# Attention and soft mixture of experts on one core: every place in the written order drawn anew, and the dummy products ahead of the weights' product

## The chip, the core and the metric

The kernel runs on one core of a Trainium2 chip. The core has five engines with a queue each: PE (matrix products), DVE and POOL (vector work), ACT (scalar functions, here exponentials and copies with a cast) and SP, which here only starts transfers. The metric is the device time of one execution in microseconds (us), as the median of several runs. Every time below is of the kernel before.

## The reference, cut to what matters

For each of 4 batches there are 12,288 queries of 128 channels. The keys and values are the same 768 vectors: 12,288 inputs averaged in blocks of 4 x 4 and multiplied by a 128 x 128 matrix.

```python
kv_pool = kv.reshape(B, H // r, r, W // r, r, C).mean(axis=(2, 4))
k = v = kv_pool.reshape(B, -1, C) @ w_sr
s = scale * (q @ k.transpose(0, 2, 1))
a = np.exp(s - s.max(-1, keepdims=True)); a /= a.sum(-1, keepdims=True) + 1e-09
x = (a @ v).reshape(B * S, C)
logits = x @ phi                                  # 32 slots
d = np.exp(logits - logits.max(0)); d /= d.sum(0) + 1e-09
slot_in = d.T @ x                                 # over all 49,152 rows
slot_out = (per expert: relu(slot_in @ w1) @ w2)  # 8 experts of 4 slots
c = np.exp(logits - logits.max(1, keepdims=True)); c /= c.sum(1, keepdims=True) + 1e-09
out = c @ slot_out
```

The second softmax goes over all rows of all batches, so the result can only be written once every query has been seen. The kernel needs the attention output x only through its logits and through slot_in, and never forms it: it works from the probabilities.

## The kernel before, in words

The 49,152 queries are 384 tiles of 128, and 12 tiles make a group: 32 groups, g0 to g31, 8 to a batch. Of tile number i in a group (0 to 11) these steps are made:

- **s** (L499 to L501, PE): six products of 128 x 384, the scores of 128 queries against 768 keys, in three passes (high and low parts of both sides).
- **m** (L505, L506, DVE): the row maximum of the scores. **e** (L514, ACT): the exponential with its row sums.
- Half of each tile's probabilities is turned for the next product by DVE (**tr**, L538), the other half is cut into a high half-precision part on ACT for two tiles at once (**hi**, L521), a low part on POOL (**lo**, L525) and turned by a transposing transfer from SP (**pd**, L534, into the tile pb). hi5 serves the tiles 10 and 11, and lo10, lo11, pd10 and pd11 follow it.

Of a group:

- **LA** and **LB** (L575, L587, PE): the logits from the two halves. LB reads pb, so it needs the group's last transposing transfer to have landed.
- **lev** (L596, L598): copies of the sums out of the accumulator; **lsel** (L604, PE) puts them together; **ltr** (L613, DVE) turns them; **ln** (L632, POOL) divides by the row sums.
- **mcol** (L638, DVE) and **mmm** (L644, PE): the column maximum over the group; **mred** (L649, L659, DVE): the running maximum. **dsub** (L665, POOL), **dexp** (L702, ACT), **dmul** (L710, POOL): the weights of the second softmax.
- **T0** to **T5** (L725, PE): these weights times the probabilities, two tiles in each piece, accumulated by **tacc** (L736, DVE).
- **cmax**, **csub**, **cexp** (L741, L744, L747): the numerators of the third softmax, kept or spilled.

The steps of a group are spread over the two groups that follow: while PE does the scores of group g it does LA, LB and lsel of g-1 and the T pieces of g-1 and g-2. During a batch the keys of the next one are made: loads (L352), adds on POOL and DVE (L356), products and their evictions (**kmm** L364, **khi** L367, **klo** L371, **umm** L379, **vmm** L424). After the last group come the experts and the output.

The head, before the first tile, loads the first batch's inputs in two halves, pools them on POOL and DVE (L296, L300), and makes the keys: **hkmm0** and **hkmm1** (L364) for the two halves, **hkx** (L467) for two pieces that skip the pooling adds, **hklo0** and **hklo1** (L371) on DVE. **hfla** is 50 products of the identity with itself into a bank that nobody reads (L265). **hw** is one product of the layer's matrix with phi (L276), and **hwo** its eviction on ACT.

The order on PE, DVE, ACT and POOL is written out by hand: each step is recorded with a time `at` (the tile that it belongs to) and a kind, and the table TAU holds a number for each kind. The steps are issued in the order of the sum; a step never comes ahead of one that it needs:

```python
key = at + TAU.get(kind, 0.0)
for d in deps:
    key = max(key, self.ops[d][2] + 1e-4)
...
for n in sorted(range(len(self.ops)), key=lambda n: (self.ops[n][2], n)):
    self.ops[n][4]()
```

Kinds with an `a` ahead stand for the first group of the program, with `y` and `z` for the last two, where they differ. SP is not under this order: the framework places its transfers. A step that waits holds back everything behind it on its engine.

Of the kernel before, what the change touches and what calls it, by code (L numbers as in the profile page):

```python
# [31 lines left out]
    "ka9": -265.483, "am2": -228.979, "ka26": -228.315, "ka27": -216.005, "hkx1": -210.101, "wl6": -205.889,  # L32
    "aT5": -200.576, "aql2": -199.988, "cmul3": -193.632, "kv1": -192.138, "hkhi0": -189.577, "alo5": -188.166,
    "klo1": -184.904, "am4": -184.036, "am11": -176.431, "am6": -174.783, "cmul7": -173.78, "cmul13": -166.529,
    "crec24": -162.887, "alev0": -161.94, "humm1": -160.171, "ka28": -158.796, "hlad": -153.938, "atr2": -149.703,
    "apd9": -145.014, "hlat1": -141.493, "cmul9": -140.13, "csum13": -136.466, "hklo0": -129.179, "ka4": -128.974,
    "as8": -128.908, "aLB2": -126.414, "hqh": -126.33, "humax": -125.006, "as11": -122.356, "ahi1": -121.758,
    "humm0": -121.346, "hkx2": -121.032, "ka21": -120.235, "umm1": -119.793, "atr1": -116.116, "alo1": -114.554,
    "crec9": -113.922, "ceps12": -113.76, "am7": -113.033, "crec21": -112.6, "csum28": -111.014, "ceps30": -108.21,
    "cmul11": -106.687, "ka8": -104.178, "apd1": -102.343, "xho12": -102.266, "wl4": -102.002, "xht14": -99.953,  # L40
    "apd4": -99.229, "csum12": -97.996, "as1": -96.721, "hkmm0": -95.947, "wl3": -95.195, "aql1": -94.09,
    "ka20": -92.708, "admul": -92.617, "alo4": -91.302, "ae3": -91.262, "ahi4": -90.444, "s7": -89.221,
    "ys7": -89.221, "apd5": -88.975, "kd3": -88.752, "zs7": -88.656, "amcol": -87.304, "aqd1": -87.275, "m2": -86.508,
    "zm2": -86.508, "ym2": -86.384, "alo3": -83.039, "ae8": -82.636, "e7": -82.523, "ye7": -82.523, "ze7": -82.367,
    "ka10": -81.698, "huout": -81.585, "aLB0": -80.918, "ae10": -80.428, "cmul17": -80.252, "ahi3": -79.401,
    "xso22": -78.357, "alo11": -77.577, "ahi5": -77.082, "s1": -76.481, "zs1": -76.481, "pd2": -76.281,
    "ypd2": -76.281, "zpd2": -76.281, "ka5": -76.232, "cmul2": -76.128, "m6": -75.891, "ym6": -75.891, "ys1": -75.891,
    "husc": -74.638, "zm6": -74.521, "alo7": -73.738, "csum1": -73.624, "ceps13": -73.102, "hfla": -70.294,
    "ae5": -69.588, "ka13": -67.698, "csum22": -67.308, "csum0": -65.39, "am1": -65.188, "as3": -64.589,
    "amred": -63.833, "lev1": -63.476, "ylev1": -63.476, "zlev1": -63.476, "cb1": -62.918, "csum27": -62.889,  # L50
    "cmul15": -62.49, "hvout0": -61.708, "as5": -59.277, "ceps25": -59.027, "hkmm1": -57.375, "wl5": -54.296,
    "zs0": -54.296, "s0": -54.234, "ys0": -54.044, "as0": -53.451, "adexp": -53.316, "cmul16": -53.122,
    "am10": -52.657, "ceps9": -52.634, "ceps1": -52.622, "ae6": -51.993, "wl0": -51.933, "ceps31": -51.12,
# [114 lines left out]
def attention_then_soft_moe(ctx: ExitStack, tc: tile.TileContext, E, qT, kv0, kvT, w_sr, w_srT, phi, w1, w2, outT, spill):  # L168
# [78 lines left out]
    op = plan.op  # L247
# [5 lines left out]
    pT = pm.tile([P, 512], F32, tag="pT", name="pT")  # L253
# [24 lines left out]
    def w_out():  # L278
        nc.scalar.activation(
            wp4, D.pop("pw")[:, :NS].unsqueeze(1).broadcast_to([P, NQD, NS]), AF.Copy, scale=1.0 / R2  # L280
        )

    a = op("PE", "hw", -90, [], w_mm, acq=[("x", "pw")])
    ops_w = op("ACT", "hwo", -90, [a], w_out, use=[("x", "pw")])

    raw = {}
# [817 lines left out]
    a = None  # L1104
# [119 lines left out]
```

## Time and profile before

| what | value |
| --- | --- |
| time, median of 3 runs | 949.61 us (948.67 to 954.53) |
| the profiled execution | 953.79 us, of which the trace spans 952.0 us |
| PE busy | 860.9 us (90% of the span) |
| DVE, POOL, ACT busy | 792.9, 697.4, 667.0 us (83%, 73%, 70%) |
| mean granted clock of PE | 0.98 of 2.4 GHz |
| transposing transfers | 384, median 3.2 us from issue to landing |

Busy time is an average over stages. The head takes about the first 48 us, the main loop with its 31 groups runs to about 840 us, the last group's end, the experts and the output follow. In a row of waits the engine and line that waited stand first, and behind the arrow what ended last before it could go on; "issue" there means that the profile names nothing. A transfer's duration on SP is only the time that its issue takes; when its data has landed is told apart.

### The profile page before, as it was taken

How to read it: one execution, taken by the hardware profiler on the slowest of the kernel's cores; microseconds unless marked ns; L12 is line 12 of the kernel's file. 1: busy time of each engine (PE TensorE's matmuls, PEld its weight loads, DVE VectorE, ACT ScalarE, POOL GpSimd, SP SyncE). 2: the span in 40 equal slices, each digit the busy share in tenths (PEclk: the TensorE clock that was granted, in tenths of full speed). 3: DMA queues.
4: the chain of work that ended last, by engine and by line, in shares of the span. 5: the costliest groups of instructions: out<-in, count | busy, mean ns of one | idle time of the engine just before them, and what ended most of it. 6: DMA issues, size and time to landing. Idle time of an engine off the chain costs nothing. (4 is left out here: it accounts for less than half of the span.)

```text
span 952.0 us, 27485 instructions
## 1 busy us (share of the span) xinstructions
PE 860.9 (90%) x10616; PEld 634.1 (67%) x10616; DVE 792.9 (83%) x1497; ACT 667.0 (70%) x1253; POOL 697.4 (73%) x822
## 2 busy tenths in 40 slices
PE   6798999989999999989999999899999999967882
PEld 6666776766777776657777777667777777744341
DVE  3887898988998988889999989888989798945891
ACT  1586787867887777767888778767878787831562
POOL 4377799886788888876787989957877677746530
PEclk9999999999999999999999999999999999989985
DMA  8377798997888899866888889867867767697699
GB/s 322 98 129 140 134 183 194 179 170 143 148 160 169 174 169 201 168 135 131 154 162 154 165 180 173 157 108 135 131 133 135 122 127 139 114 257 291 275 412 374
DMA packets 338867, 167.64 MB, mean 176 GB/s; under 512 B 310832, under 2 KB 313648, under 8 KB 338608
## 3 DMA queue, kind: packets, MB, share of 16 engines
q1 hardware_dynamic: 337728, 162.59, 79.2%
q10 hardware_dynamic: 1008, 3.29, 0.9%
q8 instruction: 83, 1.36, 0.6%
q14 instruction: 48, 0.39, 0.1%
HBM read 62.01 MB, written 28.31 MB: 95 GB/s over the span
## 5 line engine op out<-in xcount | busy, mean ns | idle before, releaser
L514 ACT ACTIVATE p<-s,nm 128x768 f32<-128x768 f32 x384 | 344.1, 897 | 124.6 <-DVE nm L506 113.6
L525 POOL TENSOR_TENSOR hl<-p,hl 128x384 f16<-128x384 f32 x384 | 347.6, 926 | 75.9 <-ACT hl L521 75.7
L505 DVE TENSOR_REDUCE nm<-s 128x1 f32<-128x768 f32 x384 | 363.6, 947 | 30.3 <-PE s L501 29.5
L499 PE MATMUL s<-khi,qhi 128*128 128x384 f32 x768 | 280.2, 365 | 8.1 <-ACT p L514 5.7
L501 PE MATMUL s<-khi,qlo 128*128 128x384 f32 x768 | 258.7, 337 | 0.2 <-POOL qlo L483 0.2
L500 PE MATMUL s<-klo,qhi 128*128 128x384 f32 x768 | 258.0, 336 | 0.2 <-DVE klo L371 0.2
L499 PEld LDWEIGHTS s<-khi,qhi 128*128 128x128 f32 x768 | 143.9, 187 | 75.0 <-issue 42.3
L538 DVE STREAM_TRANSPOSE pa<-p 128x768 f32<-128x768 f32 x192 | 176.7, 945 | 0.5 <-ACT p L514 0.2
L521 ACT ACTIVATE hl<-p 128x768 f16<-128x768 f32 x192 | 157.5, 836 | 17.0 <-DMA pb<-hl 13.8
L725 PE MATMUL pT<-p,D 128*32 128x192 f32 x3072 | 146.0, 332 | 2.8 <-POOL D L710 2.5
L500 PEld LDWEIGHTS s<-klo,qhi 128*128 128x128 f32 x768 | 144.5, 188 | 1.1 <-DVE klo L371 0.4
L501 PEld LDWEIGHTS s<-khi,qlo 128*128 128x128 f32 x768 | 144.1, 188 | 0.6 <-POOL qlo L483 0.5
L483 POOL TENSOR_TENSOR qlo<-q,qhi 128x512 fp32r<-128x512 f32 x96 | 124.7, 1299 | 5.8 <-ACT qhi L479 5.8
L725 PEld LDWEIGHTS pT<-p,D 128*32 128x32 f32 x3072 | 91.1, 110 | 44.4 <-POOL D L710 11.0
L575 PE MATMUL lq<-pa,vu 32*32 32x384 f32 x3072 | 88.4, 491 | 2.7 <-ACT hl L521 2.4
L587 PE MATMUL lq<-pb,vb 128*32 128x384 f16 x1152 | 56.1, 339 | 22.3 <-DMA pb<-hl 14.7
L514 ACT ACTIVATION_READ_ACCUMULATOR p<-s,nm 128x1 f32 x384 | 74.1, 193 | 0.0
L506 DVE TENSOR_SCALAR nm<-nm 128x1 f32<-128x1 f32 x384 | 59.0, 154 | 13.2
L598 DVE COPY lps<-lq 128x768 f32<-128x768 f32 x32 | 30.7, 958 | 47.0 <-PE lq L587 47.0
L356 POOL TENSOR_TENSOR LL<-LL 128x384 f32<-128x384 f32 x66 | 65.1, 1010 | 5.1 <-DVE LL L356 5.1
L632 POOL TENSOR_TENSOR LL<-LL,ri 128x384 f32<-128x384 f32 x32 | 26.6, 833 | 56.5 <-DVE LL L613 37.5
L587 PEld LDWEIGHTS <-vb 128*32 128x32 f16 x1152 | 30.3, 99 | 56.3 <-issue 36.6
(131 smaller groups left out, 822.4 us busy)
## 6 DMA issues: line engine op xcount, KB each, us to landing
q<-qT SPq DMA_DIRECT2D x96, 256.0 KB, 3.1
outT<-o SPq DMA_DIRECT2D x32, 768.0 KB, 11.1
LL<-kvT SPq DMA_DIRECT2D x48, 384.0 KB, 3.8
pb<-hl SPq DMA_TRANSPOSE x384, 3.2
raw<-kv SPq DMA_DIRECT2D x6, 768.0 KB, 7.9
w_p<-w SPq DMA_DIRECT2D x6, 768.0 KB, 7.4
pa<-w SPq DMA_DIRECT2D x1, 3328.0 KB, 16.7
spill<-LL SPq DMA_DIRECT2D x16, 192.0 KB, 3.5
```

Of the source, the lines that this page charges most:

```text
L483: nc.gpsimd.tensor_tensor(out=lo, in0=src, in1=hi.bitcast(F32), op=ALU.subtract)
L499: nc.tensor.matmul(s, hi[:, qc], khi[:, k], start=True, stop=False)
L500: nc.tensor.matmul(s, hi[:, qc], klo[:, k], start=False, stop=False)
L501: nc.tensor.matmul(s, lo[:, qc], khi[:, k], start=False, stop=True)
L505: nc.vector.tensor_reduce(out=NM[t], in_=S[t][:, :, :HK], axis=XY, op=ALU.max, negate=True)
L514: nc.scalar.activation(PP[t // 2][:, t % 2, :].rearrange("p (h n) -> p h n", h=2), S.pop(t)[:, :, :HK], AF.Exp, bias=NM.pop(t), scale=1.0, ...
L521: nc.scalar.activation(HL[k][:, :, 0, :], PP[k][:, :, KA:], AF.Copy)
L525: nc.gpsimd.tensor_tensor(out=hl[:, 1, :], in0=PP[t // 2][:, t % 2, KA:], in1=hl[:, 0, :], op=ALU.subtract)
L538: nc.vector.transpose(out=PA[:, n, :, o : o + 2, :].rearrange("p n a i -> p a n i"), in_=PP[k][:, :, :KA].rearrange("p a (n j) -> p a n j" ...
L575: nc.tensor.matmul(lp(g, c, r), VU[b][rows, kb, :], PA[rows, halves(g), kb, :, :], start=(k == 0), stop=False, skip_group_check=True)
L587: nc.tensor.matmul(lp(g, c, r), VB[b][:, w, kb, :], PB[:, halves(g), p * NBB + kb, :, r * Q32 : (r + 1) * Q32], start=False, stop=(n + NQD ...
L725: nc.tensor.matmul(d["pst"][c * Q32 : (c + 1) * Q32, :KW], d["D"][:, t, :], pp[:, u, c * KW : (c + 1) * KW], start=(t == 0), stop=(t == G ...
```

## The change

It does two things. All numbers of TAU are replaced, so most steps stand in another place; the numbers were found by a search that reckons with a longer landing of the transposing transfers. And in the head the 50 dummy products are issued first on PE, with the weights' product hw behind them (it now depends on them), where hw was first before. No step is added or taken away, and no step's shape changes. In the changed kernel line numbers are 19 higher from the table's end to the new lines, and 20 higher behind them.

```diff
 TAU = {
-    "ka9": -265.483, "am2": -228.979, "ka26": -228.315, "ka27": -216.005, "hkx1": -210.101, "wl6": -205.889,
...
+    "crec24": -162.887, "crec21": -112.6, "csum28": -111.014, "ceps30": -108.21, "ae3": -85.272053, "cmul17": -80.252,
...
-    a = op("PE", "hw", -90, [], w_mm, acq=[("x", "pw")])
+    a = op("PE", "hfla", 0, [], lambda: fill(pT, 50), acq=[("T", "f0")])
+    a = op("PE", "hw", -90, [a], w_mm, acq=[("x", "pw")])
     ops_w = op("ACT", "hwo", -90, [a], w_out, use=[("x", "pw")])
...
-    op("PE", "hfla", 0, [], lambda: fill(pT, 50), acq=[("T", "f0")])
+
     kv_ops(0, 0, [[pool0[0]], [pool0[1]]], [("p", "po0")], "h")
```

Three places matter for what follows.

First, DVE in a group in the middle of the loop, from the maxima that follow LB to mred. L505 and L506 are one tile's maximum (s is its scores), L613 ltr, L638 and L639 mcol, L649 and L659 mred. Before:

```order
699 L505 TENSOR_REDUCE nm_6308<-s_6299 128x1
700 L506 TENSOR_SCALAR nm_6308<-nm_6308 128x1
701 L613 STREAM_TRANSPOSE LL<-px 128x384
702 L505 TENSOR_REDUCE nm_6331<-s_6324 128x1
703 L506 TENSOR_SCALAR nm_6331<-nm_6331 128x1
704 L638 TENSOR_REDUCE cq_6348<-LL 128x12
705 L639 TENSOR_REDUCE cm_6349<-cq_6348 128x1
706 L505 TENSOR_REDUCE nm_6370<-s_6334 128x1
707 L506 TENSOR_SCALAR nm_6370<-nm_6370 128x1
708 L649 TENSOR_REDUCE gm_6380<-px 128x32
709 L659 TENSOR_TENSOR gm_6380<-gm_6380,gm_6011 128x32
```

Now (L525 and L526 the maximum, L633 ltr, L658 and L659 mcol, L669 and L679 mred, L643 the reciprocals that ln needs):

```order
701 L525 TENSOR_REDUCE nm_6312<-s_6305 128x1
702 L526 TENSOR_SCALAR nm_6312<-nm_6312 128x1
703 L643 RECIPROCAL ri_6315<-r_5681 128x12
704 L633 STREAM_TRANSPOSE LL<-px 128x384
705 L525 TENSOR_REDUCE nm_6341<-s_6334 128x1
706 L526 TENSOR_SCALAR nm_6341<-nm_6341 128x1
707 L658 TENSOR_REDUCE cq_6348<-LL 128x12
708 L659 TENSOR_REDUCE cm_6349<-cq_6348 128x1
709 L525 TENSOR_REDUCE nm_6365<-s_6358 128x1
710 L526 TENSOR_SCALAR nm_6365<-nm_6365 128x1
711 L669 TENSOR_REDUCE gm_6376<-px 128x32
712 L679 TENSOR_TENSOR gm_6376<-gm_6376,gm_6009 128x32
```

The pattern is the same, but each of ltr, mcol and mred now stands behind the maximum of a tile one later: 8, 9 and 10 where it was 7, 8 and 9. On PE the same shift shows as LB, s6, s7, s8, lsel, s9, s10, s11, mmm, T4, T5, s0, s1, T0, where it was LB, s6, s7, lsel, s8, s9, s10, mmm, T4, T5, s11, s0, s1, T0 (T4 and T5 of the group before, s0 and s1 of the group after). So T0 stands two tiles behind mmm and no longer three.

Second, POOL in the same group, from dsub to the lows of the last tiles. L525 is a low part (x2: two tiles), L665 dsub, L710 dmul, L483 a query's low part, L744 csub, L619 a step of the row sums. Before:

```order
311 L665 TENSOR_TENSOR D_6383<-LL,gm_6380 128x384
312 L525 TENSOR_TENSOR hl_6373<-p_6306,hl_6373 128x384
313 L710 TENSOR_TENSOR D_6383<-D_6383,ri_6186 128x384
314 L525 TENSOR_TENSOR hl_6401<-p_6388,hl_6401 128x384 x2
315 L483 TENSOR_TENSOR qlo_6430<-q_6322,qhi_6429 128x512
316 L744 TENSOR_TENSOR LL<-LL,RM 128x384
317 L619 TENSOR_SCALAR r_6074<-r_6074 128x12
318 L525 TENSOR_TENSOR hl_6451<-p_6391,hl_6451 128x384 x2
```

Now (L685 dsub, L545 the lows, L730 dmul, L503 the query's low part, L639 the row sums):

```order
286 L685 TENSOR_TENSOR D_6012<-LL,gm_6009 128x384
287 L545 TENSOR_TENSOR hl_6035<-p_5959,hl_6035 128x384
288 L730 TENSOR_TENSOR D_6012<-D_6012,ri_5948 128x384
289 L639 TENSOR_SCALAR r_5681<-r_5681 128x12
290 L545 TENSOR_TENSOR hl_6035<-p_5959,hl_6035 128x384
291 L503 TENSOR_TENSOR qlo_6047<-q_5989,qhi_6046 128x512
292 L545 TENSOR_TENSOR hl_6054<-p_6037,hl_6054 128x384 x2
```

Between dsub and dmul stands lo8 where lo7 stood, and between dmul and the last pair lo10, lo11 (the last row of each piece) stand one low, a query's part and a short step; the two lows of tiles 8 and 9 and csub are gone from there. On ACT hi5, which the last pair needs, stands right behind e11 and a query's part, ahead of e0 and e1 of the next group; it stood behind them before.

Third, DVE in the head, the pooling adds (L296, L300 before, L316, L320 now) and the low parts of the keys (L371 before, L391 now). Before:

```order
9 L296 TENSOR_TENSOR pooled_189<-raw_0_110 128x384
10 L371 SCALAR_TENSOR_TENSOR klo_192<-pk_193,khi_191 128x384
11 L296 TENSOR_TENSOR raw_0_120<-raw_0_120,raw_1_122 128x768
12 L300 TENSOR_TENSOR raw_2_124<-raw_2_124 128x768
13 L296 TENSOR_TENSOR raw_0_120<-raw_0_120,raw_2_124 128x768
14 L296 TENSOR_TENSOR pooled_189<-raw_0_120 128x384
15 L300 TENSOR_TENSOR raw_3_126<-raw_3_126 128x768
16 L296 TENSOR_TENSOR pooled_189<-pooled_189,raw_3_126 128x384
17 L371 SCALAR_TENSOR_TENSOR klo_192<-pk_193,khi_191 128x384
```

Now:

```order
9 L316 TENSOR_TENSOR pooled_184<-raw_0_103 128x384
10 L316 TENSOR_TENSOR raw_0_113<-raw_0_113,raw_1_115 128x768
11 L320 TENSOR_TENSOR raw_2_117<-raw_2_117 128x768
12 L316 TENSOR_TENSOR raw_0_113<-raw_0_113,raw_2_117 128x768
13 L316 TENSOR_TENSOR pooled_184<-raw_0_113 128x384
14 L391 SCALAR_TENSOR_TENSOR klo_187<-pk_188,khi_186 128x384
15 L320 TENSOR_TENSOR raw_3_119<-raw_3_119 128x768
16 L316 TENSOR_TENSOR pooled_184<-pooled_184,raw_3_119 128x384
17 L391 SCALAR_TENSOR_TENSOR klo_187<-pk_188,khi_186 128x384
```

The low part of the first half's keys now stands behind four of the second half's adds.

At the end of the loop PE's order was mmm of g30, T4, T5, s11 of g31, T0 to T3 of g30, LA and LB of g31, lsel, T4, T5, mmm; it now is T4, T5, s10, s11, mmm, LA0, T0 to T5 of g30, the rest of LA, LB, lsel, mmm. LB of g31 thus has all six T pieces of g30 ahead of it instead of four. On DVE the step mred of g30 there stands behind tacc, tr3 and the maxima of the tiles 10 and 11, where it stood behind the maxima of 9 and 10. Of the loads of the experts' weights (L976) one stands ahead of the last two transposing transfers where two stood. In the loop the last add of the next batch's keys on DVE stands behind the maximum of tile 11 in both, but the scores of tile 11 come ahead of mmm now; and the products vmm come a group later.

## Rows read from the trace of the kernel before

**Rows 1.** window of the main loop; us, then busy us (instructions) per engine
```profile
48.00:840.00 792.00, 751.47 (x9693) 565.26 (x9696) 700.46 (x1305) 613.52 (x1171) 637.23 (x725) 1.00 0.81 152
```

**Rows 2.** waits of PE, 48 to 840; us in total, times, longest
```profile
PE lq L587 <- DMA pb<-hl: 10.1, 7, 2.4
PE lq L587 <- issue: 6.4, 6, 1.4
PE s L499 <- ACT p L514: 4.7, 14, 0.9
PE pu L379 <- DVE LL L356: 4.2, 3, 1.4
PE pk L364 <- ACT khi L367: 2.7, 3, 0.9
```

**Rows 3.** timeline of PE, 798 to 803; start, us, instruction, [idle before <- releaser]
```profile
802.29 1.16 PE L587 MATMUL lq<-pb,vb 128*32 128x384 f16 x24 [1.03 <-issue]
```

**Rows 4.** timeline of PE, 822 to 828
```profile
825.67 1.65 PE L587 MATMUL lq<-pb,vb 128*32 128x384 f16 x36
```

**Rows 5.** tile pb in 797.5 to 798.9, one transpose: issue to landing
```profile
DMA to landing us min/median/max: 4.5/4.5/4.5
```

**Rows 6.** tile pb in 822.0 to 823.4, one transpose: issue to landing
```profile
DMA to landing us min/median/max: 2.8/2.8/2.8
```

**Rows 7.** timeline of PE, 448 to 466
```profile
454.81 0.85 PE L604 MATMUL px<-lps,selb 128*32 128x384 f32 x8
...
458.82 0.49 PE L644 MATMUL px<-ident,cm 128*128 128x128 f32 x2
...
464.05 1.51 PE L725 MATMUL pT<-p,D 128*32 128x192 f32 x32
```

**Rows 8.** timeline of POOL, 448 to 476
```profile
460.66 1.02 POOL L665 TENSOR_TENSOR D<-LL,gm 128x384 f32<-128x384 f32 x1 [0.19 <-DVE gm L659]
461.62 0.93 POOL L525 TENSOR_TENSOR hl<-p,hl 128x384 f16<-128x384 f32 x1
463.15 0.83 POOL L710 TENSOR_TENSOR D<-D,ri 128x384 f32<-128x384 f32 x1 [0.60 <-ACT D L702]
...
468.37 1.80 POOL L525 TENSOR_TENSOR hl<-p,hl 128x384 f16<-128x384 f32 x2 [0.39 <-ACT hl L521]
```

**Rows 9.** timeline of ACT, 448 to 476
```profile
461.66 0.90 ACT L514 ACTIVATE p<-s,nm 128x768 f32<-128x768 f32 x1 [0.76 <-DVE nm L506]
...
462.56 0.52 ACT L702 ACTIVATE D<-D 128x384 f32<-128x384 f32 x1
...
467.45 0.83 ACT L521 ACTIVATE hl<-p 128x768 f16<-128x768 f32 x1
```

**Rows 10.** timeline of PE, start to 34
```profile
8.80 13.75 PE L265 MATMUL pT<-ident 128*128 128x128 f32 x100
22.39 0.81 PE L364 MATMUL pk<-pooled,w_sb 128*128 128x384 f32 x2
...
28.76 0.91 PE L364 MATMUL pk<-pooled,w_sb 128*128 128x384 f32 x2 [1.54 <-DVE pooled L296]
```

**Rows 11.** timeline of DVE, start to 34
```profile
1.32 0.29 DVE L221 TENSOR_REDUCE mask<-ident 128x8 f32<-128x128 f32 x1 [1.32 <-POOL ident masks.py:199]
...
14.69 2.05 DVE L296 TENSOR_TENSOR pooled<-raw 128x384 f32<-128x384 f32 x1
23.76 0.56 DVE L371 SCALAR_TENSOR_TENSOR klo<-pk,khi 128x384 fp32r<-128x384 f32 x1 [7.02 <-ACT khi L367]
...
30.23 0.56 DVE L371 SCALAR_TENSOR_TENSOR klo<-pk,khi 128x384 fp32r<-128x384 f32 x1
```

**Rows 12.** timeline of PE, 833 to 869
```profile
838.79 4.48 PE L725 MATMUL pT<-p,D 128*32 128x192 f32 x64 [2.04 <-POOL D L710]
...
850.59 3.00 PE L587 MATMUL lq<-pb,vb 128*32 128x384 f16 x36 [4.62 <-DMA pb<-hl]
```

**Rows 13.** windows around a fall of the PE clock (PEclk)
```profile
88.80:92.20 3.40, 3.13 (x37) 0.50 1.03 240
```

## What was predicted

> **What bounds the kernel now.** I read the stages first: in the main loop PE is busy for 751.5 of 792.0 us [rows 1]. PE is the bound there, and what a new order can win in the loop is at most the 40.5 us in which PE stands still. The list of PE's waits over the same stretch says where they are [rows 2]. The largest is LB (L587): 10.1 us in which the profile names the transposing transfer and 6.4 us under "issue"; a single wait of 1.1 us, put down to a load, has the same cause, so 17.6 us. The two timeline rows of LB show the pattern: in g29 LB starts after a gap of 1.03 us [rows 3], in g30 without one [rows 4]. The difference is the landing of the last transfer: 4.5 us after its issue in g29 [rows 5], 2.8 in g30 [rows 6]. So the order gives the last transfer room for 2.8 us and not for 4.5. By the counts behind the sums there are 14 such waits, the longest 2.4 us. Next come the scores on an exponential (4.7 us), the umm product on DVE's key adds (4.2, three times) and kmm on an eviction (2.7) [rows 2].
>
> **The transfers' wait.** hi5 is issued in the new order ahead of e0 and e1, which stood ahead of it: two exponentials of 0.90 and 0.19 us with their row sums [rows 9], 2.2 us. lo10 and lo11 follow it on POOL (1.80 us for two [rows 8]) and the transfers behind them on SP, whose order keeps them as a pair with a query load behind, not ahead. In rows 3 and 5 the last transfer is 1.0 us too late; 2.2 us earlier leaves 1.2 us to spare. So I cost LB's wait at nothing: -17.6 us. The bounds: none of it goes (0), all of it (-17.6).
>
> **The new wait.** From lsel (454.81) to T0 (464.05) it takes 9.24 us, and T0 starts just 0.07 us after dmul has ended (463.15 + 0.83) with no idle time [rows 7, 8]. That chain has no slack against PE's stream. The change puts lsel one tile later and leaves T0 where it is in the stream. A tile of scores is 1.05 us: three fill the time from lsel's end (455.66) to mmm (458.82) [rows 7]. So T0 would come 1.05 us late, unless the chain shortens. It does between dsub and dmul, which started 2.49 us apart: dsub had ended at 461.68, but dexp only started at 462.56, since an exponential of 0.90 us stood ahead of it [rows 8, 9]. In the new order that exponential's maximum comes ahead of mred, it is through before dsub ends, and dexp (0.52 us) can follow dsub at once. Then lo8 alone sets dmul's start: 0.96 us from dsub's start to the low's and 0.93 for the low [rows 8] make 1.89, 0.60 less than before. 1.05 - 0.60 = 0.45 us. The maxima ahead of ltr, mcol and mred only change places one for one, so I leave those steps as they are. Queued behind T0 on PE are T1 and the scores of the next tiles; the maxima and exponentials that follow shift along. Over 28 groups with this pattern 12.6 us. Bounds: 0, if the chain closes on DVE, and 1.05 us a group, 29 us, if dexp is held as before.
>
> **The keys of the next batch.** umm waits 1.4 us three times for DVE's last add [rows 2]. With tile 11's scores issued a tile (1.05 us) earlier the maximum ahead of that add comes earlier by as much: -3.0. kmm's wait for khi I put from 2.7 to 1.5, since its eviction stands one exponential (0.90 us) less deep in one of the batches: -1.2. The moved vmm and the loads lie beside PE's work. Bounds: -6.9 (both gone) to +3 (a further umm-like wait of 1.0 in three batches).
>
> **The granted clock.** After the longest of LB's waits, 2.4 us in g1, PE worked 3.13 us at a granted clock of 0.50, the 1.2 GHz level [rows 13]. Without the wait I expect no fall there: half of 3.13, -1.6. Bounds: 0 to -1.6.
>
> **The head.** hkmm0 starts at 22.39, although its input was ready at 14.69 + 2.05 = 16.74: the dummy products, 13.75 us from 8.80 on, stood ahead of it [rows 10, 11]. They began at 8.80 only because hw stood ahead and waited for phi. The identity is there at 1.32 [rows 11], so they now run from about 1.4 to 15.2; hw follows, and hkmm0 starts at 16.8. That is 5.6 us earlier. DVE stood still for 7.02 us ahead of hklo0 at 23.76 [rows 11]; now it goes on with the second half's adds. From hklo0's end (24.32) to hkmm1 (28.76), which waits for them, they took 4.4 us [rows 10, 11]. Started at 16.74 they would be through at 21.2 if that half's loads never held them; if all simply shifts with hkmm0, hkmm1 comes at 28.76 - 5.6 = 23.2. The loads do hold some of them, and hklo0 stands among them, so I take the later end and a tile of scores' time (1.05) on top, 24.3, and hklo1 (30.23 [rows 11]) near 25.9: -4.3 us for the first scores. Of it 1.3 us are lost again, because the evictions of the values come later, behind more of ACT's first exponentials: -3.0. Bounds: -5.6 to +1.
>
> **The end.** T0 of g30 waits 2.04 us for dmul, LB of g31 4.62 us for the transfers, and then runs 3.00 us at the low clock instead of 1.65 [rows 4, 12]. In the new order there are two T pieces more, 1.51 us for the two [rows 7], ahead of LB, and the weights' loads stand behind the transfers but for one. But mmm of g30 comes a tile or two later and mred of g30 stands behind two maxima, tacc and tr3, so T0 of g30 will wait near 6 us instead of 2.04. What LB saves, up to 4.6 + 1.35, T0 (+4.0) and the T pieces (+1.5) almost take back: -1.0 with rounding. Bounds: -5 to +4.
>
> **The sum.** -17.6 + 12.6 - 4.2 - 1.6 - 3.0 - 1.0 = -14.8 us. The profiled execution took 953.79 us and lies 4.2 above the median; against it the sum gives 939.0. The runs shown are about their median of 949.61, and the waits are the same kind there: 949.61 - 14.8 = 934.8, rounded 935.
>
> **Rivals.**
>
> *T0 does not wait (922).* The replay of DVE is exact to some tenths. If the chain closes without the 0.45, 12.6 us more are won: 934.8 - 12.6 = 922. For it: the chain has no more steps than before. Against it: it had no slack before and lost 1.05. Chance 0.13.
>
> *The transfers still land late (944).* If half of LB's wait stays because landings grow where a query load falls beside them, 8.8 us are missing: 934.8 + 8.8 = 944. For it: g31's transfer shows that landings grow with other loads in flight, LB waited 4.62 us [rows 12]. Against it: 1.2 us of room at the longest usual landing. Chance 0.15.
>
> *T0's wait eats it, slower (959 and above).* Without T0's wait the gain is 27.4 us. T0 stands for 28 groups, so at 27.4 / 28 = 0.98 us a group nothing is left, and from 1.32 us a group the kernel is over 1% slower. The place is POOL's queue: dmul stands behind lo8, lo8 behind hi4 on ACT, hi4 behind an exponential. One exponential and its row sum (1.09 us) that holds hi4 makes 0.45 + 1.09 = 1.54 us a group, 934.8 + 28 x 1.09 = 965. For it: dexp was already seen behind an exponential [rows 9]. Against it: the new order has hi4 ahead of that one. Chance 0.08; 0.09 more for a wait between 0.7 and 1.3 us, which ends between 942 and 959.
>
> *The head runs at the low clock (940).* The dummy products end before hkmm0 now, and PE then stands still for 1.6 us and again while DVE adds, where before it went straight from the dummies to hkmm0 [rows 10]. The trace has a fall after a stop of 2.45 us [rows 13]. PE's own work there is at most the time from hkmm0 to hkmm1 less the wait, 28.76 - 22.39 - 1.54 = 4.8 us [rows 10]; at half speed it takes as much more: 940. The Trainium skill, "TensorE: Matmul & The Clock Gate", Part 1, calls the low clock the default that activity releases and idleness brings back; by it this rival is the likelier the longer the stops, and rows 13 agree with a fall after a stop. Against it: behind the stop of 1.54 us ahead of hkmm1 the product took 0.91 us for its pair, little over the 0.81 of hkmm0 straight behind the dummies [rows 10], so that stop brought no fall. Chance 0.05.
>
> **The numbers.** The likeliest case, T0's wait between 0.2 and 0.7 us, has 0.50 and spans 928 to 942. The range for 8 in 10 takes in T0 without a wait (922) and the lower half of the case between 942 and 959: 921 to 949. About 1% (9.5 us, so below 940.1 or above 959.1) is what can be told from no change here. Faster: 0.47 of the likeliest case, 0.13, 0.04 of the late transfers, 0.03 of the head: 0.67. Slower: 0.08. The rest, 0.25, within 1%.
>
> **What would show it.** LB's idle time in the loop falls from 17.6 us to under 2. T0 (L745 now) starts with 0.2 to 0.7 us of idle time in most groups, released by POOL's D; near zero means the first rival, above 1 us the third. hkmm0 starts near 17 and the first scores near 25, the granted clock at 1.0 in between. T0 of g30 waits 5 to 7 us and LB of g31 under 2. umm's waits are under 0.5 us. The prediction is wrong if LB's waits stay, if T0 waits over 1 us, or if a wait that no row above has, on DVE or in the scores, takes 10 us or more.

## The result and the profile after

The changed kernel takes 920.13 us (median of 4 runs, 917.64 to 921.37) against 952.07 for the kernel before on the same chip (948.67 to 957.95); the ratio is 0.9655, 95% interval 0.9597 to 0.9713. The sign was right and the size was not: -32 us where -14.8 was predicted, and 920.13 lies just below the range. The profiled execution took 921.37 us and spans 919.6, against 952.0 before: 32.4 us to account for.

Stages first: the window of the main loop, columns as in [rows 1], and one from its end.

```profile
48.00:809.00 761.00, 746.10 (x9681) 567.85 (x9679) 687.33 (x1303) 622.58 (x1168) 633.67 (x721) 1.00 0.84 157
810.00:814.00 4.00, 3.08 (x52) 1.29 (x56) 3.30 (x9) 1.26 (x2) 3.20 (x6) 0.59 0.89 154
```

PE stands still for 14.9 us in the loop, where it was 40.5 [rows 1]. The waits of PE in that window (us in total, times, longest) answer to [rows 2]:

```profile
PE s L519 <- ACT p L534: 3.4, 7, 0.8
PE pv L444 <- ACT v L447: 2.0, 3, 0.7
PE pk L384 <- ACT khi L387: 1.7, 3, 0.6
PE s L519 <- ACT us L415: 1.7, 2, 1.5
PE pT L745 <- POOL D L730: 1.3, 2, 0.9
PE px L664 <- DVE cm L659: 0.6, 1, 0.6
```

LB (L607 now) and umm are gone from the list. LB of two late groups, g29 and g30, in the timeline of PE, neither with idle time; they answer to [rows 3, 4]. Below, the landing of the transfers of g29 (the tile pb, 766 to 768):

```profile
773.08 1.65 PE L607 MATMUL lq<-pb,vb 128*32 128x384 f16 x36
...
796.51 1.65 PE L607 MATMUL lq<-pb,vb 128*32 128x384 f16 x36
```
```profile
DMA to landing us min/median/max: 3.2/3.2/3.2
```

The new wait that the prediction feared, T0's, shows in a group of the loop's middle, here g16. PE from lsel to T0, then POOL and ACT of the same group; they answer to [rows 7 to 9]:

```profile
461.09 0.85 PE L624 MATMUL px<-lps,selb 128*32 128x384 f32 x8
465.10 0.49 PE L664 MATMUL px<-ident,cm 128*128 128x128 f32 x2
...
469.41 1.51 PE L745 MATMUL pT<-p,D 128*32 128x192 f32 x32
```
```profile
466.67 1.01 POOL L685 TENSOR_TENSOR D<-LL,gm 128x384 f32<-128x384 f32 x1 [0.63 <-DVE gm L679]
467.64 0.92 POOL L545 TENSOR_TENSOR hl<-p,hl 128x384 f16<-128x384 f32 x1
468.52 0.83 POOL L730 TENSOR_TENSOR D<-D,ri 128x384 f32<-128x384 f32 x1
```
```profile
467.71 0.53 ACT L722 ACTIVATE D<-D 128x384 f32<-128x384 f32 x1 [0.28 <-POOL D L685]
468.14 0.89 ACT L534 ACTIVATE p<-s,nm 128x768 f32<-128x768 f32 x1
...
469.54 0.83 ACT L541 ACTIVATE hl<-p 128x768 f16<-128x768 f32 x1
470.30 0.90 ACT L534 ACTIVATE p<-s,nm 128x768 f32<-128x768 f32 x1
```

From lsel to T0 it is 8.32 us, 9.24 before: the chain lost 0.92 of the 1.05 us that it had to lose, and T0 has no idle time. dsub to dmul is 1.85 us as predicted (1.89). On ACT e11 stands at 468.14, hi5 at 469.54, e0 of the next group behind it.

An account of the 32.4 us. Idle rows undercount, because the ends of matmuls are modelled; so I charge each product on PE with the time from the start of the product ahead of it to its own start. A stop thus belongs to the line that had to wait, and the sum over a line's products is what the line holds. From LA of g0 to LA of g30 that is 762.12 us before and 731.08 after:

| place | before | after | change | predicted |
| --- | --- | --- | --- | --- |
| LB | 72.34 | 51.92 | -20.4 | -17.6 (wait), -1.6 (clock) |
| T pieces | 129.53 | 133.14 | +3.6 | +12.6 |
| umm and kmm | 15.83 | 10.31 | -5.5 | -4.2 |
| scores | 419.36 | 411.46 | -7.9 | 0 |
| LA | 79.61 | 78.23 | -1.4 | 0 |
| all else in the loop | | | +0.6 | 0 |
| head, to LA of g0 (60.85, 62.73) | | | +1.9 | -3.0 |
| LA of g30 to the output's first product | | | -3.2 | -1.0 |

The prediction's clock term stands with LB, because the products that ran at the low clock of [rows 13] are those of LB in g1. This is its row in the timeline of PE of the kernel before; they took 3.07 us where [rows 4] have 1.65:

```profile
89.07 3.07 PE L587 MATMUL lq<-pb,vb 128*32 128x384 f16 x36 [2.45 <-DMA pb<-hl]
```

The head went the wrong way. PE, DVE and ACT there, answering to [rows 10, 11]:

```profile
1.34 13.26 PE L284 MATMUL pT<-ident 128*128 128x128 f32 x100 [1.34 <-POOL ident masks.py:199]
...
16.15 0.91 PE L384 MATMUL pk<-pooled,w_sb 128*128 128x384 f32 x2 [1.41 <-DVE pooled L316]
...
23.02 4.21 PE L487 MATMUL pk<-raw,w_sb 128*128 128x384 f32 x6 [2.42 <-DVE klo L391]
27.02 1.48 PE L384 MATMUL pk<-pooled,w_sb 128*128 128x384 f32 x2
27.73 1.09 PE L519 MATMUL s<-khi,qhi 128*128 128x384 f32 x1
...
45.93 1.83 PE L444 MATMUL pv<-w_sb,pooled 128*96 128x128 f32 x8 [3.44 <-ACT v L447]
```
```profile
22.40 0.56 DVE L391 SCALAR_TENSOR_TENSOR klo<-pk,khi 128x384 fp32r<-128x384 f32 x1 [1.20 <-ACT khi L387]
...
29.06 0.56 DVE L391 SCALAR_TENSOR_TENSOR klo<-pk,khi 128x384 fp32r<-128x384 f32 x1
```
```profile
21.36 0.63 ACT L499 ACTIVATE qhi<-q 128x512 fp32r<-128x512 f32 x1 [6.30 <-DMA q<-qT]
21.90 0.47 ACT L387 ACTIVATE khi<-pk 128x384 fp32r<-128x384 f32 x1
```

hkmm0 comes 6.2 us sooner, as foreseen. But khi0 then stands on ACT behind the first query's conversion, which waited 6.30 us for its load, since that load now stands behind the raw ones on SP. hklo0 starts at 22.40 and holds the rest of hkx, and after that stop of 2.42 us PE's products take double: 4.21 us for six. So the first scores come at 27.73 us, 1.5 us sooner than before (29.21) where 4.3 were forecast. On the way from there to LA of g0 another 3.4 us are lost where 1.3 were forecast: vmm (L444) waits 3.44 us for an eviction, 1.93 before, and the clock falls a second time behind that stop (0.57 from 46 to 50 us).

At the end (timeline of PE) the wait that was put at T0 of g30 stands at LA0 of g31 instead, and the granted clock falls behind it, 0.59 in the window above. T0 comes at once, and LB waits 1.59 us and runs at the high clock; it answers to [rows 12].

```profile
810.92 1.60 PE L595 MATMUL lq<-pa,vu 32*32 32x384 f32 x32 [3.45 <-DVE pa L558]
812.44 4.92 PE L745 MATMUL pT<-p,D 128*32 128x192 f32 x96
...
820.81 1.65 PE L607 MATMUL lq<-pb,vb 128*32 128x384 f16 x36 [1.59 <-DMA pb<-hl]
```

### The profile page after: what moved, and what is told of

Its sections match the earlier page's. It is cut to its first block, busy times and chain, and to the rows that moved or that the text cites. A ratio compares the mean times of both kernels' runs of the same rounds, so it can differ in the third digit from the quotient of the medians.

```text
span 919.6 us, 27400 instructions
## 1 busy us (share of the span) xinstructions
PE 856.0 (93%) x10616; PEld 633.7 (69%) x10616; DVE 779.1 (85%) x1497; ACT 677.6 (74%) x1253; POOL 697.1 (76%) x822
## 4 chain that ended last, share of the span: by engine, by line
PE 53%; DVE 18%; POOL 11%; ACT 3%; issue 3%; DMA 2%; POOLq 0%; ACTq 0%; DVEq 0%
PE s L519 10%; PE lq L595 8%; DVE nm L525 8%; PE pT L745 8%; PE s L521 8%; PE s L520 8%; PE lq L607 5%; POOL hl L545 4%; POOL D L685 3%; POOL D L730 2%; PE px L624 2%; DVE cq L658 2%; PE po L1175 2%; ACT p L534 2%; DVE nm L526 1%
## 5 line engine op out<-in xcount | busy, mean ns | idle before, releaser
L525 DVE TENSOR_REDUCE nm<-s 128x1 f32<-128x768 f32 x384 | 362.9, 945 | 41.7 <-PE s L521 41.5
L534 ACT ACTIVATE p<-s,nm 128x768 f32<-128x768 f32 x384 | 344.3, 898 | 59.5 <-DVE nm L526 46.1
L545 POOL TENSOR_TENSOR hl<-p,hl 128x384 f16<-128x384 f32 x384 | 348.8, 934 | 27.0 <-ACT hl L541 25.9
L541 ACT ACTIVATE hl<-p 128x768 f16<-128x768 f32 x192 | 160.9, 838 | 7.8 <-DMA pb<-hl 1.4
L503 POOL TENSOR_TENSOR qlo<-q,qhi 128x512 fp32r<-128x512 f32 x96 | 123.5, 1286 | 44.0 <-ACT qhi L499 39.6
L595 PE MATMUL lq<-pa,vu 32*32 32x384 f32 x3072 | 90.9, 495 | 3.5 <-DVE pa L558 3.5
L499 ACT ACTIVATE qhi<-q 128x512 fp32r<-128x512 f32 x96 | 59.8, 623 | 43.0 <-PE s L520 36.7
L526 DVE TENSOR_SCALAR nm<-nm 128x1 f32<-128x1 f32 x384 | 59.1, 154 | 13.2
L595 PEld LDWEIGHTS lq<-pa,vu 32*32 32x32 f32 x3072 | 46.1, 103 | 33.0 <-issue 8.5
L607 PE MATMUL lq<-pb,vb 128*32 128x384 f16 x1152 | 52.7, 327 | 1.6 <-DMA pb<-hl 1.6
L607 PEld LDWEIGHTS <-vb 128*32 128x32 f16 x1152 | 27.9, 96 | 33.9 <-issue 21.6
```

Of the source, the lines that this page charges most:

```text
L503: nc.gpsimd.tensor_tensor(out=lo, in0=src, in1=hi.bitcast(F32), op=ALU.subtract)
L525: nc.vector.tensor_reduce(out=NM[t], in_=S[t][:, :, :HK], axis=XY, op=ALU.max, negate=True)
L534: nc.scalar.activation(PP[t // 2][:, t % 2, :].rearrange("p (h n) -> p h n", h=2), S.pop(t)[:, :, :HK], AF.Exp, bias=NM.pop(t), scale=1.0, ...
L541: nc.scalar.activation(HL[k][:, :, 0, :], PP[k][:, :, KA:], AF.Copy)
L545: nc.gpsimd.tensor_tensor(out=hl[:, 1, :], in0=PP[t // 2][:, t % 2, KA:], in1=hl[:, 0, :], op=ALU.subtract)
L595: nc.tensor.matmul(lp(g, c, r), VU[b][rows, kb, :], PA[rows, halves(g), kb, :, :], start=(k == 0), stop=False, skip_group_check=True)
```

## The experiments

Twelve kernels ran. A diff without another name is against the changed kernel; ratios are to the kernel before on the same chip, with 95% intervals. "Loop" is LA of g0 to LA of g30, "room" the median time from the end of lo11 to the start of LB: 4.1 us before in groups without a wait, 6.1 after.

**Which place took LB's wait away.** First hi5 was put back behind e0 and e1:

```diff
-"hi5": 19.029218
+"hi5": 19.3531
```

> The changed kernel with one number of the table put so that hi5 stands behind e0 and e1 of the next group again, as before the change. If the prediction's reason holds (hi5's two places give the last transfers their room, 2.2 us), LB waits again in the 12 to 14 groups with a long landing, about 1 us each: PE's wait at LB goes from 0 to 10 to 18 us in the loop and the time to 930 to 938. Rival (the room comes from tile 11's scores, which now stand ahead of mmm, T4 and T5): POOL's queue and not hi5 sets lo11 now (hi5 ends 3.1 us ahead of lo11), so lo11 moves by under 1 us, LB's wait stays under 3 us, time 918 to 923.

924.25 us, ratio 0.9692 (0.9646 to 0.9738). LB's wait stays at zero with a room of 5.04 us; mmm waits 4.7 us instead of 0.6. Only about 4 of the 32 us hang on hi5 here (the loop is 5.4 us longer in the trace; the intervals of the two ratios overlap), and its place gives 1.1 us of room where 2.2 were forecast. So the prediction's reason for LB was not the only one. The counterpart, hi5 moved alone in the kernel before:

```diff
-"hi5": 15.405
+"hi5": 14.9
```

> The kernel before with one thing of the change alone: the high half of the last tile pair (hi5) ahead of the two exponentials e0 and e1 that stood ahead of it; all other orders are those of before. The prediction's step taken alone: between the changed kernel and the one with hi5 put back, the room from the last low half (lo11) to LB differed by 1.1 us (6.14 against 5.04). Added to the 4.06 us that a group without a wait has in before, that is some 5.1 us, more than a landing of 4.5: LB's wait falls from 17.6 us to under 2 and the time by about 17, to some 935. Rival, that the waits at LB, mmm, LA and umm are one slack shared in a group: LB's wait falls, but most of it comes back at the scores, whose exponentials e0 and e1 are now later by 0.8 us, or at mmm and LA, and the time falls by less than 10, to 943 or above.

950.0 us, ratio 0.9978 (0.9947 to 1.001): no gain that can be told. Yet LB lost its wait as the prediction said: room 4.95 us, LB from 72.34 to 52.35 us with no idle time in any group of the loop. The rival had it right, for the waits of PE in its loop now begin with the scores:

```profile
PE s L499 <- ACT p L514: 13.6, 37, 2.5
```

These were 4.7 us in 14 times [rows 2]; with what follows each stop, the scores hold 15.0 us more than before, out of the 20.0 that LB gave. The rows of one such wait, on ACT (e11, hi5, e0) and on PE (T0, and the scores of the fourth tile):

```profile
459.59 0.88 ACT L514 ACTIVATE p<-s,nm 128x768 f32<-128x768 f32 x1
460.38 0.19 ACT L514 ACTIVATION_READ_ACCUMULATOR p<-s,nm 128x1 f32 x1
460.60 0.84 ACT L521 ACTIVATE hl<-p 128x768 f16<-128x768 f32 x1
461.35 0.88 ACT L514 ACTIVATE p<-s,nm 128x768 f32<-128x768 f32 x1
```
```profile
459.40 1.51 PE L725 MATMUL pT<-p,D 128*32 128x192 f32 x32
...
462.38 0.44 PE L499 MATMUL s<-khi,qhi 128*128 128x384 f32 x1 [0.23 <-ACT p L514]
```

The fourth tile's scores (s3) start when e0, three tiles back, has ended. They are due 2.6 us after T0's start. Measured over 26 groups, e0 ended 1.96 us after it in the kernel before (median), 2.84 in this one, 1.75 in the changed one. There e11 ended 0.38 us ahead of T0, not 1.08 behind it. The place of tile 11's scores ahead of mmm is not what this hangs on alone: in the next run they stand behind mmm again, and still e11 ends 0.10 us ahead of T0, e0 2.03 behind it, and from g2 on s3 has no stop. On ACT, hi4 and a query's part stood between dexp and e11 before and no longer do. That order, as I read it, lets hi5 stand ahead of e0 at no cost; it was not tested alone.

Nor does this run show that hi5's place alone gives enough room. In the kernel before, the last transfer of a group took 4.0 to 4.7 us to land in 12 of the groups g1 to g30; here it took 3.8 at most, and half of the added room (0.4 of 0.9 us) comes from LB, which s3's stop makes later. In the changed kernel long landings are left and the room does cover them: in seven groups the last transfer took 4.4 to 4.7 us and had landed 0.9 to 1.6 us ahead of LB. With the old room, 2 us less, each of these would have come late.

**The order of PE and DVE.** Four entries were set so that PE has lsel, s8, s9, s10, mmm, T4, T5, s11 again, and DVE the maximum of tile 10 behind mred:

```diff
+TAU.update({"s8": 15.25, "s9": 15.75, "m10": 16.4, "s11": 18.0})
```

> The changed kernel with four numbers of the table put so that PE and DVE in the middle groups have the order of before again (lsel ahead of s8, s11 behind mmm, T4 and T5, with the maxima and reductions that follow them), while ACT and POOL keep the new order. Unlike the run that moved s11 alone, lsel is a tile earlier too, so mmm should not wait. Theory: two moves give the transfers their room, tile 11's scores (1.75 us) and hi5's place (1.8 us, of which POOL's queue takes 1.2 back), and either alone is nearly enough. Then lo11 ends 4.7 to 5.9 us ahead of LB (6.1 in the changed kernel, 4.06 before): LB waits 0 to 6 us in the loop, T0 not at all, umm 2 to 4 us again: 918 to 928. Rival (the order of PE and DVE is the whole of the gain): LB waits 12 us or more, 935 to 950.

940.5 us, ratio 0.9886 (0.985 to 0.9923). LB waits for nothing here either (room 6.25 us), but 20 us of the gain are gone: mmm holds 8.5 us more, LA 7.2, the scores 5.6, umm 3.4; T gives 3.0 back. So most of the gain hangs on the order of PE and DVE, of which I had priced only T0's loss. Of the scores, those of the second tile (s1) hold 8.7 us more than in the changed kernel; their stops wait for an exponential. With hi5 put back as well:

```diff
+TAU.update({"s8": 15.25, "s9": 15.75, "m10": 16.4, "s11": 18.0, "hi5": 19.3531})
```

> The run before with hi5 put behind e0 and e1 again as well, so both moves are undone. Theory: lo11 ends 3.5 to 4.3 us ahead of LB, as before the change (4.06), LB waits about 1 us or more in the groups with a long landing: 12 to 30 us in the loop, 935 to 950. Rival (POOL's new order alone gives the room): LB's wait under 6 us, 918 to 928.

951.2 us, ratio 0.9995 (0.9977 to 1.0013): the whole gain is gone with five of the table's 753 entries (94 of which the change had left as they were). Whether these five alone would win it in the kernel before was not run. And the wait does not return to LB. Waits of PE in the loop:

```profile
PE px L665 <- DVE cm L660: 16.3, 15, 2.3
...
PE lq L608 <- DMA pb<-hl: 0.8, 3, 0.4
```

It stands at mmm. ln, two steps ahead of mmm on POOL, starts 2.9 us after lsel in the mean, 2.1 in the changed kernel and 2.6 with the four entries alone: POOL gets to it late, coming straight from other work in 23 of 29 groups (7 in the changed kernel). The room at LB is 4.89 us, in groups with a stop at mmm and without one alike, so these stops do not make it; lo11 ends 5.6 us behind T0 of the group before where it was 6.1, by entries that are still the new ones. One slack that shows at whichever place PE reaches first would fit these waits, but no run shows it.

To bring the wait back to LB, the DVE turn tr3 was also put ahead of the maximum of tile 11, as in the kernel before:

```diff
-TAU.update({"s8": 15.25, "s9": 15.75, "m10": 16.4, "s11": 18.0, "hi5": 19.3531})
+TAU.update({"s8": 15.25, "s9": 15.75, "m10": 16.4, "s11": 18.0, "hi5": 19.3531, "tr3": 17.7})
```

> The run that had PE's and DVE's old order and hi5 behind e0 and e1, with a third thing undone: the transposition tr3 stands ahead of the maximum of tile 11 on DVE again, as before the change. Theory: the room of the last transfers has two sources that came out of the runs so far, hi5's place and the maximum of tile 11 ahead of tr3 (0.93 us). With hi5 alone undone lo11 ended 4.9 to 5.0 us ahead of LB, just enough for the long landings; with both it ends 3.6 to 4.2 ahead (4.06 before the change) and LB waits again, 0.6 us or more in the groups with a long landing: 5 to 17 us in the loop, 950 to 962. Rival (the waits at mmm have given LB its room for good): LB's wait stays under 2 us, time 948 to 953.

954.66 us, ratio 1.0016 (0.9983 to 1.0048). The room is 4.71 us and LB waits 3.0 us in all: less than was expected, and mmm still waits 18.2. Which entry moved the wait from LB to mmm is open.

Tile 11's scores alone put back, lsel left where the change has it:

```diff
-"s11": 4.618826
+"s11": 18.0
```

> The changed kernel with one number of the table put so that the scores of tile 11 stand behind mmm, T4 and T5 again, as before the change. If the place of tile 11's scores gives the transfers their room: LB waits about 1 us in the groups with a long landing again, 8 to 18 us in the loop, and umm waits for DVE's adds up to 1.4 us in three batches; T0 gains a tile and waits no more (-2 us). Time 930 to 945. Rival (hi5's place gives the room): LB's wait stays under 3 us, time 918 to 924.

954.55 us, ratio 1.0019 (0.9993 to 1.0044). LB does not wait, against what was expected; the gain is lost at mmm, which holds 29.2 us more than in the changed kernel, and at LA, 13.1 more, while T and the scores give 8.3 back. Waits of PE in the loop:

```profile
PE px L664 <- DVE cm L659: 26.1, 29, 1.0
```

lsel to mmm is 4.02 us through DVE and POOL in all these kernels where nothing is late. With s11 gone from that stretch, two tiles are left to fill it, and mmm waits 0.9 us in every group.

**Why T0 hardly waits.** An idle add of the size of a low part was put on POOL ahead of dsub, beside mred's second step, in groups 1 to 29:

```diff
+    dum = cp.tile([P, 384], F32, tag="dum", name="dum")
+    nc.gpsimd.memset(dum, 0.0)
...
+            if 0 < g < NG - 2:
+                op("POOL", "dum", at + 28.2, [], lambda: nc.gpsimd.tensor_tensor(out=dum, in0=dum, in1=dum, op=ALU.add))
```

> The changed kernel with one more POOL instruction (an add of 128 x 384 on a scratch tile) between lo7 and dsub in the groups 1 to 29. Theory: T0 did not wait because POOL now stands idle ahead of dsub, so that mred's second step takes 0.19 us (0.5 before, beside a query's low part on POOL) and dsub follows at once. With the dummy POOL is busy for about 0.9 us from lo7's end: mred's second step is stretched to 0.4 to 0.7 us, dsub comes 0.4 later, T0 waits 0.4 to 0.6 us instead of 0.09 in each group, time +9 to +15 (929 to 935). Rival (T0's chain closes on ACT and DVE, POOL has room): mred keeps 0.19 us or T0 still waits under 0.2, time within 3 us of the changed kernel.

929.72 us, ratio 0.9766 (0.9718 to 0.9813). mred's second step on DVE, duration min/median/max in ns: before, after, and in this kernel.

```profile
L659 DVE TENSOR_TENSOR gm<-gm,gm x31: 192/513/946, 99.7 to 858.8; 128x32 f32<-128x32 f32 x31
```
```profile
L679 DVE TENSOR_TENSOR gm<-gm,gm x31: 191/192/219, 99.8 to 827.8; 128x32 f32<-128x32 f32 x31
```
```profile
L681 DVE TENSOR_TENSOR gm<-gm,gm x31: 191/545/876, 96.5 to 835.2; 128x32 f32<-128x32 f32 x31
```

The wait of T0 returned: T holds 10.6 us more than in the changed kernel. The waits of PE:

```profile
PE pT L747 <- POOL D L732: 14.2, 27, 0.8
```

In the new order POOL is idle when mred's second step starts in 26 of 31 groups, and the step takes 0.19 us instead of 0.51. In the kernel before POOL was at work then in all 31, and each time the step ended 0.05 us behind POOL's instruction. dsub follows the step's end after 0.14 us in the median in all three kernels, so the added instruction held dsub through DVE and not by standing ahead of it on POOL. The Trainium skill, "SBUF — State Buffer", "Who interferes with whom", says that a DVE instruction with two inputs in SBUF contends with a GpSimd instruction that reads SBUF; these three rows agree.

As a counter-test dmul was put ahead of lo8 on POOL, to take away what is left of T0's wait:

```diff
+TAU.update({"lo8": 18.1})
```

> The changed kernel with dmul ahead of lo8 on POOL. Theory: dmul now follows dexp (0.53 us) and not the low (0.92), it starts 0.3 us earlier, and the last 0.09 us of wait at T0 in each group go: T0's waits fall from 3.6 to under 1 us in the loop, time 916.5 to 919.5. Rival: lo8 and the lows behind it come 0.8 us later and the scores wait for them through hi's tiles or the transfers: no gain or up to 5 us slower.

921.06 us, ratio 0.9675 (0.9609 to 0.974): no gain. T holds 4.3 us less, mmm 3.5 and LA 1.3 more; ln starts 0.2 us later in the mean. What T gave, mmm and LA took.

**The head.** The old order of the first two steps in the changed kernel, then the new one in the kernel before:

```diff
-    a = op("PE", "hfla", 0, [], lambda: fill(pT, 50), acq=[("T", "f0")])
-    a = op("PE", "hw", -90, [a], w_mm, acq=[("x", "pw")])
+    a = op("PE", "hw", -90, [], w_mm, acq=[("x", "pw")])
...
+    op("PE", "hfla", 0, [], lambda: fill(pT, 50), acq=[("T", "f0")])
```

> The changed kernel with the weights' product ahead of the 50 dummy products again, as before the change; the new table stays. Theory: in the new table's head nothing is won by the dummies' place, since the second half's loads and adds on DVE set it, and the early dummies let the clock fall: the first scores come within 1.5 us of the changed kernel's (26.5 to 27.7 in the runs so far), at a granted clock of 1.0, LA of g0 up to 2 us earlier, time 917 to 921. Rival (the early dummies win 3 to 5 us as predicted): the first scores come at 30 or later, time 922 to 926.

```diff
-    a = op("PE", "hw", -90, [], w_mm, acq=[("x", "pw")])
+    a = op("PE", "hfla", 0, [], lambda: fill(pT, 50), acq=[("T", "f0")])
+    a = op("PE", "hw", -90, [a], w_mm, acq=[("x", "pw")])
...
-    op("PE", "hfla", 0, [], lambda: fill(pT, 50), acq=[("T", "f0")])
```

> The kernel before with the 50 dummy products ahead of the weights' product and nothing else changed (old table; the low part of the first keys stands ahead of the second half's adds on DVE there). Theory: the first product of the keys comes at 16.8 instead of 22.4, the first keys' low part at 18, the adds then run until 23 to 24, first scores at 24 to 25.5 instead of 29.2, LA of g0 3 to 5 us earlier: ratio 0.995 to 0.997. Rival (loads and adds set the head in any order): first scores move by under 1.5 us, ratio 0.999 to 1.001.

920.84 us with the dummies behind (ratio 0.9674, 0.9637 to 0.9712), LA of g0 at 62.31 us: with the new table, the early dummies win nothing. In the kernel before they do: LA of g0 at 56.8 instead of 60.9 us, 950.08 us, ratio 0.996 (0.9928 to 0.9992). The two parts of the change work against each other in the head. Two trials to mend it, first the first query's load alone ahead of the raw ones:

```diff
-    ops["q", 0] = op("SP", "qd0", -90, [], lambda: q_load(0), acq=[("q", 0)])
+    ops["q", 0] = op("SP", "qd0", -95, [], lambda: q_load(0), acq=[("q", 0)])
```

> The changed kernel with the load of the first queries issued on SP ahead of the twelve loads of the first keys, as before the change. Theory: in the changed kernel this load lands behind them near 21 us, ACT waits for it with the first queries' high part, and the first keys' evictions khi0 and klo0 and so hkx wait behind it; PE stands still for 2.4 us and falls to the 1.2 GHz level. With the load first, khi0 comes 1.0 to 1.5 us earlier, PE's stop ahead of hkx is under 1.5 us and the granted clock in 20 to 30 us stays at 1.0; first scores 2.5 to 4.5 us earlier, time 915.5 to 918. Rival (the second half's loads and adds set the head): first scores move by under 1 us, low clock as before, time as the changed kernel's.

921.53 us, ratio 0.9669 (0.9632 to 0.9707); the first scores start at 29.5 us, later than the 27.7 of the changed kernel. The load did go first: the framework places SP's transfers, but a step's number moves them too. POOL's low parts of the queries came earlier, beside DVE's adds. DVE and POOL of this kernel:

```profile
19.14 2.00 DVE L316 TENSOR_TENSOR raw<-raw,raw 128x768 f32<-128x768 f32 x1 [2.33 <-POOL raw L320]
...
23.03 1.50 DVE L316 TENSOR_TENSOR pooled<-raw 128x384 f32<-128x384 f32 x1
```
```profile
19.06 1.26 POOL L503 TENSOR_TENSOR qlo<-q,qhi 128x512 fp32r<-128x512 f32 x1
...
22.44 1.68 POOL L503 TENSOR_TENSOR qlo<-q,qhi 128x512 fp32r<-128x512 f32 x1 [2.12 <-ACT qhi L499]
```

The two adds took 0.96 and 0.56 us in the changed kernel. hklo0, behind them on DVE, came at 24.46. Second, the same load with the kernel before's order of khi0, klo0, hkx and the query's conversion:

```diff
+TAU.update({"hkhi0": -189.577, "hklo0": -129.179, "hkx0": -0.916, "hqh": -126.33})
...
-    ops["q", 0] = op("SP", "qd0", -90, [], lambda: q_load(0), acq=[("q", 0)])
+    ops["q", 0] = op("SP", "qd0", -95, [], lambda: q_load(0), acq=[("q", 0)])
```

> The changed kernel with the head's order of before in four steps and one load: the first keys' low part hklo0 ahead of the second half's adds on DVE, khi0 ahead of hkx on PE's side (hkx behind hklo0), the first queries' high part first on ACT, their load first on SP. The dummies stay first. Theory: on the old table the early dummies brought LA of g0 from 60.9 to 56.8; on the new one nothing, because khi0 waits for hkx (its input lands at 19 to 20 us), and hklo0 stands behind adds that wait for loads. With the old order first scores at 24.5 to 25.5 (26.5 to 27.7 now), granted clock 1.0 until then, LA of g0 at 58 to 60.5 (62.3 to 62.7 now): 915 to 918. Rival (loads and DVE's adds set it anyway): LA of g0 stays above 61.5, 919 to 921.

915.82 us (913.69 to 917.35), ratio 0.9613 (0.9558 to 0.9668): 4.3 us better than the changed kernel by the medians, with its slowest run below the changed kernel's fastest, the best of all that ran. Its head on PE:

```profile
16.67 0.91 PE L385 MATMUL pk<-pooled,w_sb 128*128 128x384 f32 x2 [1.49 <-DVE pooled L317]
...
20.24 2.82 PE L488 MATMUL pk<-raw,w_sb 128*128 128x384 f32 x8 [2.01 <-DMA raw<-kv]
24.73 0.91 PE L385 MATMUL pk<-pooled,w_sb 128*128 128x384 f32 x2 [1.67 <-DVE pooled L317]
25.18 0.64 PE L520 MATMUL s<-khi,qhi 128*128 128x384 f32 x1
```

All of hkx runs in one piece at the high clock, since klo0 is through before it (18.14 us on DVE), and the scores start at 25.18 us instead of 27.73. LA of g0 comes at 59.5 instead of 62.7. The windows from 20 to 30 us, changed kernel and this one:

```profile
20.00:30.00 10.00, 7.43 (x16) 3.97 (x14) 4.15 (x7) 2.02 (x4) 2.49 (x2) 0.66 0.46 161
```
```profile
20.00:30.00 10.00, 7.38 (x25) 4.40 (x26) 9.45 (x14) 2.15 (x5) 2.47 (x3) 1.00 0.52 174
```

Granted clock 0.66 against 1.00, with the same busy time and more products done.

## Why the prediction was wrong in size

**The step that failed** is the new wait, T0's +12.6 us. It measured +3.6 in the account, and in most groups 0.07 to 0.10 us of idle time where 0.45 was predicted. The mechanism was right, a chain from lsel to T0 without slack that had to lose 1.05 us, and so was the 0.60 between dsub and dmul. The missing term lies between mred and dsub, which I left "as they are": 0.66 us before from the start of mred's second step to dsub's (median), 0.34 after, because that step no longer runs beside POOL. The row of before that would have told it, a spread of 192 to 946 ns for one and the same instruction, had not been read. This term is 9.0 of the 17.6 us between forecast and account.

That makes the first rival, T0 without a wait at 922 us, the one that came true. That its time is off by only 2 us is luck: T0 still cost 3.6 us and the head 4.9 more than forecast, while the scores, LB, the keys, LA and the end gave some 14 us that no term had.

**A term put at nothing.** The scores' waits on exponentials stood in [rows 2] and got no term. They went from 14 to 7, and the scores hold 7.9 us less, all of it missed. By tile, 4.0 us of it lie at s1, 3.6 at s4 and s5. s1's part hangs on the order of PE and DVE, for with the old one s1's stops are back; the part of s4 and s5 is not, and its cause is open. The stops at s3 that hi5 alone brought are others: the kernel before has none there in the middle of the loop.

**LB:** right in size (-20.4 against -17.6 and -1.6), but the reason was one of several. hi5's place gave 0.9 to 1.1 us of room and not 2.2. LB's wait also stays away with hi5 put back, with the order of PE and DVE put back, and but for 1.0 us with both. What it wins depends on the order around it: hi5's place won no time that can be told in the kernel before, where the gain came back at the scores; the new order without it keeps most of the gain (924.25 us), and with the old order of PE and DVE it keeps a third (940.5).

**Keys:** -5.5 against -4.2: umm gave 4.6 of a forecast 3.0, kmm 0.9 of 1.2. umm's waits are gone; with the old order of PE and DVE 3.4 us come back, as argued, though behind an exponential and not an add.

**Head:** hkmm0's 5.6 us came (6.2), and the way through DVE's adds was misread. I moved hklo0 behind them and did not follow khi0 on ACT past a conversion that waits for a load; and the 1.3 us put on the later evictions of the values measured 3.4 between the first scores and LA of g0. The rival of the low clock in the head, chance 0.05, did occur: 0.66 in that window. With the old head order LA of g0 comes 3.3 us earlier, of which the clock is a part, so it cost less than the 4.8 put on it; the other terms outweighed it, and its 940 us did not come.

**End:** -3.2 against -1.0, where the terms as written add up to -0.5. The wait of T0 of g30 did not come; LA0 ahead of it waited 3.45 us instead, on DVE's turn.

**What stays open:** how the 20 us of the four PE and DVE entries split into causes. mmm, LA, the scores and umm share them, and each try to single out one wait moved it to another place. Open too is which of the other entries keep LB's room with the five put back.

## What to carry to other kernels

When PE is the bound and a wait is worth about a microsecond a group, do not price its removal by its own idle time alone: take the next two places where PE may stop instead, here the scores on e0 and mmm, and ask whether the same edit or another gives them room too. An instruction of one shape whose duration varies by a factor of five in the trace, as mred's second step did, may be waiting inside itself; find out beside what it is long before taking its duration into a chain. Parts of a change that are good alone can work against each other, so predict them together and test them apart.

## What the runs showed of the hardware

A short DVE instruction with two inputs in SBUF (mred's second step, 128 x 32) takes 0.19 us beside an idle POOL and 0.51 to 0.55 in the median beside a busy one, up to 0.95; in the kernel before it ended 0.05 us behind POOL's instruction in every group. A pooling add took 2.00 us instead of 0.96 beside POOL's low part of a query, ending 0.8 us after it. The trace shows this as busy time of DVE, not as a wait.

In the head of the changed kernel the granted clock fell to 0.5 behind a stop of 2.42 us and again behind one of 3.44, and PE's products took up to double; with the old head order it stayed at 1.0 behind stops of 2.01 and 1.67 us and fell behind the one of 3.44. With the dummies behind hw it stayed at 1.0 behind the same stop of 3.44 us ahead of vmm (row below). So in these runs the length of a stop does not tell by itself whether the clock falls.

```profile
47.11 1.11 PE L443 MATMUL pv<-w_sb,pooled 128*96 128x128 f32 x8 [3.44 <-ACT v L446]
```
